# Decay weights of one superblock loaded as token pairs on two queues, with a new order of steps, in a kernel of RWKV-6 attention and a SwiGLU layer

## The chip, the cores and the metric

The kernel runs on one core of a Trainium2 chip. The metric is the device time of one execution in microseconds (us), lower is better. The kernel before took 209.78 us as the median of three runs (208.58 to 213.54). The profile is that of one execution; its span, from the first to the last instruction, is about 1.7 us shorter than the time that goes with it (208.2 for 209.92). No second core can explain anything here, so a run counts as slow only if it is more than 1.5% above the fastest of its own kernel; ratios below are of fast runs, while the medians quoted are of all runs.

## The reference, cut to what matters

```python
B, H, S, D = 4, 8, 768, 48                       # r, k, v, w: (B, H, S, D) float32
for t in range(S):                               # attention: a state of D x D per batch and head
    cur = einsum('bhd,bhe->bhde', u * kt, vt)
    y[:, :, t] = einsum('bhd,bhde->bhe', rt, state + cur)
    state = wt[:, :, :, None] * state + einsum('bhd,bhe->bhde', kt, vt)
x = y as (B*S, H*D) = (3072, 384)
xn = x / rms(x) * rms_g                          # feed-forward, 384 -> 1536 -> 384
out = (silu(xn @ w_gate) * (xn @ w_val)) @ w_out
```

## The kernel before

The sequence is cut into 6 superblocks n of 128 tokens; each has the 4 batches j. For a block (n, j), 128 tokens lie on the 128 partitions. The decays w are needed as sums of logarithms over the tokens before and after each token. ACT takes the logarithm (`ln`), PE multiplies by a triangular mask (`cs_mm`), ACT takes the exponential (`exp_r`, `exp_k`), and DVE multiplies r and k with it. When the four blocks of a superblock are done, its 512 tokens go through the feed-forward: 12 times gate group, value group, Silu, product, then 4 output groups.

The program is a list of steps, `operation.n.j`, in a fixed order; each engine runs its own instructions in that order. The parts that the change touches:

```python
def load(which, n, j):                     # r, k, v: 128 x 8 runs of 48 floats (192 bytes)
    inp[which, n, j] = pin.tile([128, H, D], FP32, name=which + "t", bufs=NIN)
    dmas["load_" + which, n, j] = nc.sync.dma_start(out=inp[which, n, j], in_=... "h t d -> t h d")

def load_w(n, j):
    paired = (n, j - j % 2) in W_PAIR
    ...                                    # one tile [128, 2*384] for two batches
    if paired:                             # partition = token pair; 64 partitions for each batch
        o = t.rearrange("p (h x) -> p h x", h=H)[PD * (j % 2):PD * (j % 2) + PD]
        src = src.rearrange("h (g i) d -> g h (i d)", i=2)
    else:
        o = t.rearrange("p (b h d) -> p b h d", b=2, h=H)[:, j % 2]
        src = src.rearrange("h t d -> t h d")
    eng = nc.scalar if paired and j % 2 else nc.sync
    ... eng.dma_start(out=o, in_=src)

ones_row = const.tile([1, 128], FP32)
i3 = small.tile([KC, KC], FP32)
if W_PAIR:                                 # masks for sums over token pairs
    mp = const.tile([128, 2, 130], BF16)
    mp_b = junk[:, 0:2 * 130]...           # a tile that exists anyway
    ...                                    # two memsets, two selects, a copy, all on POOL

def cs_pair(n, j):                         # four half-height products in place of two, for two batches
    for t, o, late in ((b, 0, 1), (a, NP, 0)):
        for i in range(2):
            for c in range(2):
                rows = slice(PD * c, PD * c + PD)
                nc.tensor.matmul(t[c][:, o:o + DM]..., lhsT=mp[rows, i, late:late + L], rhs=lw[rows, n % 2, j + i, :, 0:D], ...)
```

The paired code stood in the kernel before, but `W_PAIR = ()` kept it off. In the built program the pools lie one after the other: the constants from byte 16640 of a partition, then the persistent tiles from 20736, the input tiles (`pin`) from 79104, the work tiles (`pt`) from 128256.

## Time and profile before

| | before |
|---|---|
| time, median of 3 | 209.78 us |
| PE busy, all of it | 189.6 us of the 208.2 us span |
| first gate group starts | 29.04 us |
| PE idle from there to 160 us | 130.96 - 125.85 = 5.11 us |
| hardware queue of SyncE | 125328 packets |

The prediction reads these numbers as two stages and shows the lines. In what follows, a hole is a stretch in which PE is idle after the start of the first gate group.

### The profile page before, as it was taken

What the parts mean: (1) busy time and instruction counts of PE and PEld (TensorE: products, weight loads), DVE (VectorE), ACT (ScalarE), POOL (GpSimd) and SP (SyncE); (2) the same over time, 40 slices, a digit from 0 to 9 for tenths busy, and PEclk for the clock granted to TensorE, in tenths of its full rate; (3) what the DMA queues carried; (4) which work ended last, traced back from release to release, by engine and by line L of the source; (5) the groups of instructions that cost most, each with busy time, mean ns of one, the idle gap of its engine ahead of it and who ended that gap; (6) DMA issues with size and microseconds to landing.
All of it is one profiled execution on the core that took longest, in us unless ns stands there. A gap on an engine that the chain in (4) does not pass through costs nothing.

```text
span 208.2 us, 4362 instructions
## 1 busy us (share of the span) xinstructions
PE 189.6 (91%) x1512; PEld 110.6 (53%) x1512; DVE 156.1 (75%) x314; ACT 141.0 (68%) x290; POOL 108.9 (52%) x167
## 2 busy tenths in 40 slices
PE   5666869899999999889999999999999999999994
PEld 2444524456565555555555655555555655555563
DVE  6497855799899898869989969978997956254311
ACT  3786994678997646699637998569887973344110
POOL 3398504479789498856699692566614520000000
PEclk9995579999999999999999999999999999999999
DMA  6999999999999999899999968995467130200122
GB/s 133 212 201 204 179 201 202 186 190 225 189 209 224 135 225 190 179 260 208 177 211 205 225 150 186 168 229 107 113 176 143 38 113 3 77 0 0 39 101 91
DMA packets 127391, 32.81 MB, mean 158 GB/s; under 512 B 122244, under 2 KB 126216, under 8 KB 127368
## 3 DMA queue, kind: packets, MB, share of 16 engines
q1 hardware_dynamic: 125328, 28.98, 69.4%
q0 software_dynamic: 2032, 3.54, 9.3%
q8 instruction: 12, 0.20, 0.4%
q14 instruction: 11, 0.09, 0.1%
q10 hardware_dynamic: 8, 0.00, 0.0%
HBM read 25.96 MB, written 4.72 MB: 147 GB/s over the span
## 4 chain that ended last, share of the span: by engine, by line
PE 47%; SPq 20%; ACT 10%; DMA 7%; DVE 6%; POOL 5%; issue 3%; POOLq 0%; ACTq 0%; DVEq 0%
SPq L210 16%; PE ps_q L625 14%; PE ps_a L565 14%; PE ps_b L565 13%; SPq L227 4%; DMA rt<-in_r_dram 3%; DVE ht L583 3%; DMA kt<-in_k_dram 2%; ACT xn L528 2%; DMA wt<-in_w_dram 2%; ACT L195 2%; ACT sg L197 1%; POOL rstd L524 1%; ACT junk L515 1%; ACT ps_a L197 1%
## 5 line engine op out<-in xcount | busy, mean ns | idle before, releaser
L583 DVE TENSOR_TENSOR ht<-ps_b,sg 128x512 bf16<-128x512 f32 x72 | 49.0, 687 | 21.9 <-PE ps_b L565 17.4
L197 ACT ACTIVATE sg<-ps_a 128x512 bf16<-128x512 f32 x72 | 42.6, 596 | 32.2 <-PE ps_a L565 32.1
L565 PE MATMUL ps_a<-xnt,wg_sb 128*128 128x512 bf16 x216 | 59.4, 385 | 1.0 <-DMA wg_sb<-in_moe_w_gate_dram 0.8
L565 PE MATMUL ps_b<-xnt,wv_sb 128*128 128x512 bf16 x216 | 59.2, 383 | 0.5 <-DVE ht L583 0.5
L625 PE MATMUL ps_q<-wo_sb,ht 128*128 128x384 bf16 (+1 forms) x300 | 49.9, 319 | 0.3 <-ACT ob L634 0.3
L422 POOL TENSOR_TENSOR ruk<-rt,kt 128x384 f32<-128x384 f32 x24 | 24.6, 1024 | 23.7 <-DMA rt<-in_r_dram 17.2
L625 PEld LDWEIGHTS <-ht 128*128 128x128 bf16 x300 | 28.1, 98 | 16.7 <-issue 0.2
L565 PEld LDWEIGHTS <-wg_sb 128*128 128x128 bf16 x216 | 23.4, 115 | 21.3 <-issue 1.5
L565 PEld LDWEIGHTS <-wv_sb 128*128 128x128 bf16 x216 | 23.5, 114 | 20.7 <-issue 1.4
L432 POOL TENSOR_TENSOR ydiag<-vt,diag 128x384 f32<-128x384 f32 x24 | 19.9, 830 | 10.9 <-DMA vt<-in_v_dram 6.1
L423 POOL TENSOR_TENSOR ruk<-ruk,u_bc 128x384 f32<-128x384 f32 x24 | 24.2, 1006 | 1.9
L634 ACT COPY ob<-ps_q 128x384 f32<-128x384 f32 (+1 forms) x20 | 9.2, 473 | 14.3 <-PE ps_q L625 13.7
L464 DVE TENSOR_TENSOR qts<-ps_q,mask_lt 128x512 bf16<-128x512 f32 x24 | 16.4, 682 | 1.7 <-PE ps_q L459 1.3
L197 ACT ACTIVATE lw<-wt 128x384 bf16<-128x384 f32 x24 | 12.3, 518 | 7.2 <-DMA wt<-in_w_dram 7.1
L528 ACT ACTIVATE xn<-xb,rstd 128x384 bf16<-128x384 f32 x24 | 14.4, 608 | 3.4 <-POOL rstd L524 3.3
L475 POOL TENSOR_SCALAR_AFFINE_SELECT qts<-qts 128x512 bf16<-128x512 bf16 x20 | 13.1, 655 | 6.1 <-ACT qts L468 5.9
L510 DVE TENSOR_TENSOR xb<-ps_q,ydiag 128x384 f32<-128x384 f32 x24 | 13.1, 551 | 2.4 <-PE ps_q L505 2.3
L195 ACT ACT_TABLE_LOAD x10 | 12.8, 1283 | 1.8 <-PEq L661 1.6
L515 ACT ACTIVATE junk<-xb 128x384 bf16<-128x384 f32 x24 | 12.4, 515 | 2.1 <-DVE xb L510 1.8
L416 DVE TENSOR_TENSOR rk<-kt,ps_b 128x384 bf16<-128x384 f32 x20 | 10.9, 548 | 3.6 <-ACT ps_a L197 1.8
L411 DVE TENSOR_TENSOR rk<-rt,ps_a 128x384 bf16<-128x384 f32 x20 | 10.9, 548 | 2.7 <-DMA rt<-in_r_dram 1.2
L427 DVE TENSOR_REDUCE diag<-ruk 128x8 f32<-128x384 f32 x24 | 12.9, 542 | 0.0
(71 smaller groups left out, 262.0 us busy)
## 6 DMA issues: line engine op xcount, KB each, us to landing
wt<-in_w_dram SPq DMA_DIRECT2D x24, 192.0 KB, 3.9
vt<-in_v_dram SPq DMA_DIRECT2D x24, 192.0 KB, 3.9
kt<-in_k_dram SPq DMA_DIRECT2D x24, 192.0 KB, 3.9
rt<-in_r_dram SPq DMA_DIRECT2D x24, 192.0 KB, 3.8
out_dram<-ob SPq DMA_DIRECT2D x23, 192.0 KB, 2.7
wo_sb<-in_moe_w_out_dram POOLq DMA_DIRECT2D x3, 384.0 KB, 6.3
wv_sb<-in_moe_w_val_dram POOLq DMA_DIRECT2D x1, 768.0 KB, 10.5
wg_sb<-in_moe_w_gate_dram POOLq DMA_DIRECT2D x1, 768.0 KB, 14.0
```

The source lines that it names most:

```text
L195: nc.scalar.preload_act_table_set(table_name)
L197: return nc.scalar.activation(**kw).ins
L210: dmas["load_" + which, n, j] = nc.sync.dma_start(out=inp[which, n, j], in_=t[j, :, n * L:(n + 1) * L, :].rearrange("h t d -> t h d")).ins
L422: nc.gpsimd.tensor_tensor(out=ruk[n, j], in0=inp["r", n, j], in1=inp["k", n, j], op=ALU.mult)
L423: nc.gpsimd.tensor_tensor(out=ruk[n, j], in0=ruk[n, j], in1=u_bc, op=ALU.mult)
L432: nc.gpsimd.tensor_tensor(out=ydiag[n, j], in0=inp["v", n, j], in1=diag[n, j].to_broadcast([128, H, D]), op=ALU.mult)
L464: nc.vector.tensor_tensor(out=qts[n, j][:, 0], in0=bank["q", n, j][0], in1=bc_mid(mask_lt, NP), op=ALU.mult)
L515: nc.scalar.activation(out=junk, in_=xb[n, j], func=AF.Square, accum_out=rstd[n, j][:, 0:1])
L528: nc.scalar.activation(out=xn, in_=xb[n, j], func=AF.Copy, scale=rstd[n, j][:, 1:2])
L565: nc.tensor.matmul(ps, lhsT=units(ws, c, f), rhs=xnt[n][:, c, :], start=(c == 0), stop=(c == KC - 1))
L583: nc.vector.tensor_tensor(out=ht[n][:, f, :], in0=bank.pop(("v", n, f)), in1=bank.pop(("sg", n, f)), op=ALU.mult)
L625: nc.tensor.matmul(ps[:, cols], lhsT=ht[n][:, f, b * L:(b + 1) * L], rhs=wo_sb[:, f, cols], start=(f == 0), stop=(f == FC - 1))
```

## The change

The four w loads of superblock 1 are to use 384-byte runs (two tokens that lie side by side in memory) instead of 192-byte runs, so half as many packets. The two batches of a pair go to different halves of the partitions, one issued by SyncE, one by ACT. The price is a mask for the sums over pairs, and sums in two half-height products. The whole order of steps was made anew with it.

```diff
-    W_PAIR = ()
+    W_PAIR = ((1, 0), (1, 2))
...                                        the order: a few of its lines near the first gate group
-load_r.1.0 x_add.0.1 load_gv.0.0 q_mask_e.0.2 cast_v.0.3 load_r.1.1 xn_mul.0.0 bonus_sum.0.3 load_gv.0.1 q_mm.0.3
-ln.1.2 y_mm.0.2 bonus_v.0.3 x_sq.0.1 q_mask_e.0.3 st_mm.0.1 exp_k.1.0 w_tot.0.3 x_add.0.2 load_gv.1.1 cs_mm.1.1
+cs_mm.1.0 q_mask_e.0.2 load_v.1.0 bonus_v.0.2 cast_v.0.2 x_add.0.1 ln.1.2 bonus_sum.0.3 load_r.1.1 load_gv.0.1
+st_mm.0.1 x_sq.0.1 q_mm.0.3 st_new.0.1 exp_k.1.0 load_k.1.1 xn_pe.0.0 bonus_v.0.3 exp_r.1.0 q_mask_e.0.3 y_mm.0.2
...                                        (the other lines of the order are cut)
-        for c in (j, j + 1) if n in Q_PAIR else (j,):
+        for c in (j, j + 1) if (n, j) in Q_PAIR else (j,):
```

`Q_PAIR` is empty, so the last edit does nothing. `load_gv.g.h` loads part g of the gate weights (h = 0) or value weights (h = 1).

## The prediction

> **What bounds the kernel now.** I read the page's busy tenths first (40 slices of 5.2 us), then the busy time by windows, the timeline of the first 60 us engine by engine, and the DMA view by windows.
>
> ```profile
> PE   5666869899999999889999999999999999999994
> PEclk9995579999999999999999999999999999999999
> DMA  6999999999999999899999968995467130200122
> ```
>
> TensorE (PE) is full from slice 8 on, and the DMA engines are full from 5 us to about 125 us. So there are two regimes: a head of about 30 us in which PE is fed by what the DMAs bring and runs partly at half clock, and a body in which PE itself is the bound. The windows view puts sizes to that (columns: busy us and count of PE, its weight loads, DVE, ACT, POOL; then granted clock, DMA share, GB/s):
>
> ```profile
> 16.00:20.00 4.00, 2.51 (x30) 1.71 (x28) 3.08 (x7) 2.44 (x6) 3.35 (x5) 0.50 1.02 201
> 20.00:24.00 4.00, 3.36 (x41) 2.37 (x42) 2.98 (x8) 3.92 (x13) 3.77 (x5) 0.50 1.02 169
> 24.00:28.00 4.00, 2.29 (x20) 1.21 (x19) 3.06 (x9) 3.90 (x13) 0.00 (x0) 0.85 1.23 202
> ...
> 84.00:88.00 4.00, 3.45 (x38) 2.33 (x39) 3.56 (x9) 2.82 (x7) 3.18 (x6) 1.00 0.73 145
> 88.00:92.00 4.00, 2.99 (x35) 2.00 (x33) 2.22 (x6) 3.07 (x8) 3.21 (x6) 1.00 1.13 279
> ```
>
> ACT, not PE, is full from 20 to 28 us. From 40 us to 160 us PE's idle time, summed over the 10 us windows, is 4.3 us, of which 1.6 us lies in 84 to 92. Nothing after 160 can be won except the output tail. A gate or value group of three matmuls takes 0.65 us, an output group of twelve 1.95 us: 144 x 0.65 + 24 x 1.95 = 140 us are fixed work. The end is therefore the start of the first gate group, plus fixed PE work, plus the few holes. Those moments in the timeline:
>
> ```profile
> 18.12 0.52 ACT L197 ACTIVATE lw<-wt 128x384 bf16<-128x384 f32 x1 [1.52 <-DMA wt<-in_w_dram]
> ...
> 21.93 7.68 SPq L210 DMA_DIRECT2D vt<-in_v_dram  x1
> ...
> 29.04 1.44 PE L565 MATMUL ps_a<-xnt,wg_sb 128*128 128x512 bf16 x3
> ...
> 31.16 0.60 ACT L197 ACTIVATE sg<-ps_a 128x512 bf16<-128x512 f32 x1
> ...
> 37.09 0.84 PE L565 MATMUL ps_a<-xnt,wg_sb 128*128 128x512 bf16 x3 [0.79 <-DMA wg_sb<-in_moe_w_gate_dram]
> ```
>
> ACT waited 1.52 us for w of (1,1), then was never free until the first Silu at 31.16. PE later lost 0.8 us to the second part of the gate weights. SyncE's issue at 21.93 was stuck for 7.68 us[...].
>
> [...]between 10 and 20 us
>
> ```profile
> q1 hardware_dynamic: 10562, 2.00, 101.2%
> ```
>
> is 1.012 x 160 us / 10562 = 15.3 ns for a 192-byte packet, and in 195 to 200 us, with almost only 1536-byte output rows, 0.21 x 80 us / 288 = 58 ns: eight times the bytes for 3.8 times the time. [...]the q matmuls (48 rows each, halves at partitions 0 and 64, two banks) start in pairs, at 80.64, 80.70, 80.75 and 80.81 us, so two of 128 columns cost about 57 ns. The new decay sums have that form (64 rows, two banks).
>
> **The change part by part.**
> Transfers: the four w loads of superblock 1 go from 1024 packets of 192 bytes to 512 of 384. A load now costs 1024/16 x 15.3 = 0.98 us of all engines. With the line through 15.3 and 58 ns a 384-byte packet is about 21.5 ns (estimate), 512/16 x 21.5 = 0.69 us; if only the count mattered, 0.49. Saved: 4 x 0.29 to 0.49 = 1.2 to 2.0 us, all before 22 us, in front of the weights.
>
> ACT: four Ln of 518 ns become two of 768 columns. The 1024-column copies took 1.01 us and 384-column Exp 0.47, so 0.84 ns a column, 0.84 us each: 0.4 us saved. ACT gains two issues; such issues took 0.45 to 1.2 us on SyncE in the first 15 us: +1 to +1.8 us. In the new order the Ln pair comes behind the first normalization, so the 1.52 us wait should be filled. One more Exp (0.47) goes ahead of the last normalization. I scheduled ACT by hand with these durations: the last normalized tile is ready at about 28.2 us instead of 27.4, but no fourth decay sum stands between it and the gate. First gate at 29.2 against 29.04, Silu at 31.2 against 31.16: no gain at the start (+0.2 us).
>
> PE: two 384-column sums per block become four half-height ones, two at a time: 8 full-height slots before and 8 after; the one-column sums go from 16 to 32, also in pairs. Zero on balance. Even if serial, 8 x 0.16 us[...] falls where PE had 5.7 us of 16 idle (12 to 28 us).
>
> POOL: the pair masks are two memsets, two selects and a copy, near 0.3 us each, placed where POOL waited 4.80 us. Hidden.
>
> Order: the value weights go first, then gate, gate, value. POOL issues the first gate part only behind a bonus product that needs v of (0,3), at 22.3 us by my count instead of 19.64; but the weight queue then still has value data to move, so this part should land as the second did, at 28.4, just in time. The second gate part, which held PE at 37.09, should land about where third in line did, 32.7, and the last value part is wanted a group later: -0.8 us. PE also does a transpose, q and state sum of (1,0) between the first groups, work moved forward.
> At 84 to 92 us ACT waited 1.08 and 1.02 us for w of superblock 3. The new order has w (3,1) five loads earlier and (3,2), (3,3) two earlier. I credit half of the 1.56 us hole: -0.7.
>
> Sum: +0.2 - 0.8 - 0.7 = -1.3 us on 209.78, about 208.5; I put it at 208.4, since the shorter transfers can only help the body.
>
> **The rivals.** (a) ACT's issue gets stuck, as SyncE's did for 7.68 us at 21.93. Then ACT, full from 20 us on, delays everything: +1 to +3 us, 210 to 212. Against it: both issues come near 13 and 16 us, before the weights, into an empty queue of their own. (b) The gate weights come late through POOL's wait for v of (0,3), which now has about 1.4 more loads ahead of it: the first gate slips to 30 or 31, +1 to +2 us. For it: the first part is issued 2.7 us later. Against: the weight queue is never empty. (c) The whole saving of 1.2 to 2.0 us reaches the start, and both holes close: 3 to 4 us, 206 to 207. Against: ACT, not the DMA, is full before the gate. (d) The transfers are hidden anyway and the reordering of the body costs as much as it gains: 209 to 210. For: the DMA is full for 125 us, yet PE hardly waits.
>
> **Range and chances.** The three runs of before span 208.58 to 213.54, so noise alone is a few us. 205.8 to 211.2 holds (c) almost whole, the centre, (d) and the mild half of (a) and (b). Faster by 2% means under 205.6, more than every hole I can name: 0.11. Slower means over 214, which needs (a) and (b) together: 0.06. The rest, 0.83, is within 2%.
>
> **What would show it.** Right: 2048 fewer packets on the hardware queues; a 384-byte packet near 21 ns; Ln with 768 columns near 0.84 us; first gate within 1 us of 29; no wait for gate weights near 37; 84 to 92 us fuller. Wrong: ACT's issues over 1.2 us each, a first gate that waits for its weights, half-height sums that follow one another, a gate start before 28, or new PE holes after 40 us over the old 4.3 us.

## The result, and the profile after

The kernel after took 216.85 us as the median of four runs (216.60 to 217.21), against 209.98 (208.58 to 213.54) for the kernel before in the same rounds. A ratio in this document is the mean time of one kernel's fast runs over that of the other's of the same rounds, so not quite the ratio of the medians quoted. Here it is 1.0352, with a 95% interval of 1.0297 to 1.0406 (the slow run of 213.54 is left out). The change is slower; the prediction said 208.4 us.

The page's busy tenths of the kernel after (40 slices of 5.4 us, rows as in the prediction), and its queue lines (packets, megabytes, packet time as a share of 16 engines):

```profile
PE   5583848997999999989999699899999999999994
PEclk9999965899999999999999999999999999999999
DMA  7999999999989999999999998999467111101022
...
q1 hardware_dynamic: 122224, 28.58, 77.8%
...
q10 hardware_dynamic: 1064, 0.40, 1.2%
```

and the queue of the kernel before:

```profile
q1 hardware_dynamic: 125328, 28.98, 69.4%
```

The packets went down, as intended: 122224 + 1064 against 125328 + 8 (the 8 of the ACT queue before) is 2048 fewer. Yet the time of the packets went up, from 69.4% of 208.2 us to 77.8% of 215.5 us. That is the first sign that something happened to every packet, not only to the w loads.

The busy windows of the kernel after that answer to those in the prediction:

```profile
16.00:20.00 4.00, 0.70 (x9) 0.35 (x8) 1.56 (x5) 3.42 (x8) 0.86 (x2) 1.00 1.40 189
20.00:24.00 4.00, 3.63 (x52) 2.73 (x52) 3.73 (x9) 2.32 (x4) 3.92 (x5) 1.00 1.29 174
24.00:28.00 4.00, 2.94 (x51) 1.90 (x48) 3.95 (x9) 3.41 (x11) 2.49 (x4) 1.00 0.99 150
84.00:88.00 4.00, 3.95 (x31) 2.07 (x32) 3.92 (x9) 2.36 (x6) 3.05 (x6) 1.00 1.34 203
88.00:92.00 4.00, 4.00 (x51) 2.72 (x50) 3.92 (x8) 3.95 (x7) 3.54 (x5) 1.00 1.08 164
```

PE did 0.70 us of work between 16 and 20 us, where the kernel before did 2.51. ACT, full from 20 to 28 us before, now had 2.3 us idle there. The 84 to 92 us stretch became full, as predicted. The DMA share is at or above 1 for nearly all of it, as before, and yet the throughput from 16 to 28 us is 189, 174 and 150 GB/s against 201, 169 and 202. The timeline names the waits:

```profile
18.90 0.55 DVE L416 TENSOR_TENSOR rk<-kt,ps_b 128x384 bf16<-128x384 f32 x1 [2.13 <-DMA kt<-in_k_dram]
20.37 1.03 PE L439 MATMUL ps_q<-ident,rk 128*128 128x128 bf16 x8 [1.52 <-DVE rk L411]
...
32.96 0.62 PE L565 MATMUL ps_a<-xnt,wg_sb 128*128 128x512 bf16 x1 [0.99 <-ACT ek L197]
...
34.47 0.60 ACT L197 ACTIVATE sg<-ps_a 128x512 bf16<-128x512 f32 x1 [0.23 <-PE ps_a L565]
```

Product k of superblock 0 waited 2.13 us for its input, and the transposes behind it came at 20.37 us. The first gate group starts at 32.96 us, 3.92 us later than before, and it comes singly, with other PE work between its three products.

Where the 7.3 us between the two spans (208.2 and 215.5) went can be counted with the sum of the prediction: start of the first gate group plus holes. Two stretches, from that start to 40 us and from 40 to 160 us, have this sum (us, then the busy time of each engine), before:

```profile
sum 130.96, PE 125.85 PEld 73.03 DVE 112.83 ACT 99.21 POOL 88.46; mean PE 62.93 PEld 36.52 DVE 56.42 ACT 49.61 POOL 44.23
```

and after:

```profile
sum 127.04, PE 119.82 PEld 69.88 DVE 106.45 ACT 92.43 POOL 83.62; mean PE 59.91 PEld 34.94 DVE 53.23 ACT 46.22 POOL 41.81
```

The holes grew from 5.11 to 7.22 us, by 2.1; with the 3.9 at the start that is 6.0 of the 7.3 us. So both stages lost, and what made them lose may have acted all along the run.

To find the first moment at which the two traces differ, I went back to the earliest transfers. Up to 10 us the two kernels issue the same loads in the same order, all of superblock 0, all of 192-byte runs; the first half of a pair is issued at 10.74 us by SyncE, the second at 12.71 us by ACT:

```profile
10.74 1.02 SPq L227 DMA_DIRECT2D wt<-in_w_dram  x1
...
12.71 0.68 ACTq L227 DMA_DIRECT2D wt<-in_w_dram  x1
```

The DMA view from 5 to 10 us, before:

```profile
q1 hardware_dynamic: 5708, 1.08, 109.6%
...
rt<-in_r_dram SPq DMA_DIRECT2D x2, 192.0 KB, 4.0
```

and after (last column of the load line: median us from issue to landing):

```profile
q1 hardware_dynamic: 5016, 0.95, 143.8%
...
rt<-in_r_dram SPq DMA_DIRECT2D x2, 192.0 KB, 4.8
```

The time per packet is share x 16 engines x 5 us over the count: 1.096 x 80 / 5708 = 15.4 ns before, 1.438 x 80 / 5016 = 22.9 ns after. The packet times sum to 109.6% and 143.8% of the time of the 16 engines, so on average more than one packet of an engine was under way, and this is how long a packet lasted and not what it cost an engine: the same loads moved at 216 GB/s before and at 190 after, 12% less. Neither paired loads, nor ACT's issues, nor the new order have begun to act there. What is different already is where the destination tiles lie. The mask `mp` has 2 x 130 x 2 = 520 bytes in each partition and takes 544 (it starts at 20736, the next tile at 21280), in the pool in front of everything that is allocated later. No trace shows an address, but those in the two programs, when they are built, confirm it: `wt` moved from 79104 to 79648, `vt` from 91392 to 91936, `kt` from 103680 to 104224, `rt` from 115968 to 116512. All four were multiples of 64 and are now 32 past one.

### The profile page after: what moved, and what is told of

Read it like the earlier page. It is cut to its first block, busy times and chain, and to the rows that moved or that the text cites. A ratio compares the mean times of both kernels' runs of the same rounds, so it can differ in the third digit from the quotient of the medians.

```text
span 215.5 us, 4412 instructions
## 1 busy us (share of the span) xinstructions
PE 191.3 (89%) x1519; PEld 111.9 (52%) x1536; DVE 157.8 (73%) x314; ACT 141.2 (66%) x288; POOL 109.9 (51%) x172
## 3 DMA queue, kind: packets, MB, share of 16 engines
q1 hardware_dynamic: 122224, 28.58, 77.8%
q10 hardware_dynamic: 1064, 0.40, 1.2%
## 4 chain that ended last, share of the span: by engine, by line
PE 53%; DMA 12%; ACT 12%; SPq 9%; DVE 6%; issue 4%; POOL 3%; ACTq 0%; DVEq 0%; POOLq 0%
PE ps_a L565 18%; PE ps_b L565 16%; PE ps_q L625 13%; SPq L210 5%; DMA vt<-in_v_dram 5%; DMA rt<-in_r_dram 3%; SPq L227 3%; ACT L195 2%; DMA rkT<-rk 2%; PE ps_q L457 2%; ACT xn L528 2%; DVE rk L411 2%; DMA out_dram<-ob 1%; ACT junk L515 1%; ACT lw L197 1%
## 5 line engine op out<-in xcount | busy, mean ns | idle before, releaser
L565 PE MATMUL ps_b<-xnt,wv_sb 128*128 128x512 bf16 x206 | 58.1, 384 | 1.9 <-DVE ht L583 1.6
L625 PEld LDWEIGHTS <-ht 128*128 128x128 bf16 x300 | 28.1, 98 | 17.3 <-issue 0.9
L422 POOL TENSOR_TENSOR ruk<-rt,kt 128x384 f32<-128x384 f32 x24 | 24.1, 1004 | 19.5 <-DMA kt<-in_k_dram 10.9
L475 POOL TENSOR_SCALAR_AFFINE_SELECT qts<-qts 128x512 bf16<-128x512 bf16 x20 | 12.7, 634 | 23.2 <-ACT qts L468 22.9
L197 ACT ACTIVATE lw<-wt 128x384 bf16<-128x384 f32 (+1 forms) x22 | 11.7, 545 | 4.9 <-DMA wt<-in_w_dram 4.8
L468 ACT CAST qts<-ps_q 128x512 bf16<-128x512 f32 x20 | 11.6, 582 | 4.9 <-PE ps_q L459 4.9
```

What stands on the lines that cost most here:

```text
L197: return nc.scalar.activation(**kw).ins
L422: nc.gpsimd.tensor_tensor(out=ruk[n, j], in0=inp["r", n, j], in1=inp["k", n, j], op=ALU.mult)
L565: nc.tensor.matmul(ps, lhsT=units(ws, c, f), rhs=xnt[n][:, c, :], start=(c == 0), stop=(c == KC - 1))
L625: nc.tensor.matmul(ps[:, cols], lhsT=ht[n][:, f, b * L:(b + 1) * L], rhs=wo_sb[:, f, cols], start=(f == 0), stop=(f == FC - 1))
```

## The experiments

The theory was: 192-byte packets into destinations at 32 modulo 64 are slower, and that is most of the loss. The rivals were that the loss comes from the pairs themselves (mask sums, ACT's issues, two queues), or from the new order (above all the late weight loads). Twelve kernels ran in three groups of four, each group on one chip. The kernel before took 211.72, 212.18 and 212.04 us as the median on these three chips, more than its 209.98 on the first one; the kernel after hardly differs between chips (216.85 and 217.53). Ratios below are against the kernel before of the same group. All results were correct.

| run | kernel | median us | ratio (95%) | first gate us | 192-byte packet, 5 to 10 us |
|---|---|---|---|---|---|
| e1 | after, mask padded to 1024 | 213.34 | 1.0082 (1.0018 to 1.0146) | 31.68 | 15.5 ns |
| e2 | before, shifted by 32 | 215.89 | 1.0185 (1.0128 to 1.0242) | 31.80 | 21.4 ns |
| e3 | after, mask padded to 576 | 213.14 | 1.0033 (0.9961 to 1.0104) | 32.13 | 15.3 ns |
| e4 | new order, no pairs | 212.40 | 1.0002 (0.9933 to 1.0070) | 30.75 | 15.2 ns |
| e5 | after again | 217.53 | 1.0261 (1.0194 to 1.0329) | 33.32 | 20.2 ns |
| e6 | e1, weights in the old order | 213.39 | 1.0067 (1.0003 to 1.0132) | 30.25 | 15.2 ns |
| e7 | e1, one queue | 212.62 | 1.0054 (0.9983 to 1.0126) | 31.55 | 15.2 ns |
| e8 | old order, pairs, padded mask | 215.59 | 1.0158 (1.0070 to 1.0246) | 35.32 | 15.4 ns |
| e9 | before, only load tiles shifted | 215.17 | 1.0132 (1.0091 to 1.0172) | 31.71 | 21.9 ns |
| e10 | before, all but the load tiles shifted | 212.18 | 0.9968 (0.9905 to 1.0031) | 29.31 | 15.3 ns |
| e11 | new order, weights earlier | 215.50 | 1.0125 (1.0070 to 1.0181) | 31.68 | 15.3 ns |
| e12 | before, gate part first | 212.24 | 1.0000 (0.9956 to 1.0045) | 29.48 | 15.3 ns |

Several expectations missed their ranges. The absolute times expected of e1, e3 and e4 (207 to 211 us) were missed, on a chip on which the kernel before was 2 us slower too. The ratios of e5, e8 and e11 lie outside every range that was named, and those of e9 and e10 lie just below theirs.

**e1, the mask padded.** The same kernel with 480 more bytes behind the mask, so that all later tiles move by 1024.

```diff
         mp = const.tile([128, 2, 130], BF16)
+        const.tile([128, 240], BF16, name="pad2")
```

> The changed kernel with 480 unused bytes after its new pair mask, so that every later tile moves by 1024 bytes instead of 544 and load destinations start at 0 instead of 32 modulo 64. Theory A (placement: the 520-byte mask moves all load destinations off a 64-byte boundary, and every 192-byte packet gets slower): packets between 5 and 10 us go back from 22.9 to about 15.4 ns, first gate back near 29 us, time 207 to 210 us. Theory B (the new order itself starves the gate weights): packets may change, time stays 214 or more. Theory C (the second hardware queue slows the packets): nothing changes, 217 us.

The packet time fell back to 1.115 x 80 / 5772 = 15.5 ns:

```profile
q1 hardware_dynamic: 5772, 1.09, 111.5%
```

The time is 213.34 us, ratio 1.0082. An unused pad takes back most of the loss. The first gate group didn't come back near 29 us, as theory A had it, but only to 31.68.

**e2, the kernel before shifted by 32 bytes.** Neither pairs nor the new order; 32 bytes that nobody uses in the constants.

```diff
     nc.gpsimd.memset(ones_row, 1.0)
+    const.tile([128, 16], BF16, name="pad2")
     i3 = small.tile([KC, KC], FP32)
```

> The kernel before, with nothing changed but 32 unused bytes in front of the tiles that follow the constants; load destinations start at 32 modulo 64. Theory A: packets between 5 and 10 us go from 15.4 to about 22.9 ns, time 214 to 219 us. Theories B and C: 210 us, as before.

```profile
q1 hardware_dynamic: 5056, 0.96, 135.4%
```

Packets of 1.354 x 80 / 5056 = 21.4 ns, and 1.0185 times the time (the interval lies wholly above 1, though not wholly above 2%). The pad alone makes the kernel before lose 1.8%.

**e3, the mask padded to another multiple.** 32 bytes behind the mask, so that later tiles move by 576, a multiple of 64 but not of 128 or 256.

```diff
         mp = const.tile([128, 2, 130], BF16)
+        const.tile([128, 16], BF16, name="pad2")
```

> The changed kernel with only 32 unused bytes after the mask: tiles move by 576 bytes, so destinations are at 0 modulo 64 but no longer at 0 modulo 256 as before. Theory A with a 64-byte boundary: the same as the run with 480 bytes, 207 to 210 us, packets 15.4 ns. Theory A with a wider boundary (128 or 256): between, or still 217 us. Theories B and C: 214 to 217.

Packets of 15.3 ns and a ratio of 1.0033 (one of its four runs was slow and is left out). Here it was enough that the load tiles begin at a multiple of 64 (`wt` at 79680, not a multiple of 128 or 256): the packets are as short as the 15.5 ns of e1, where they begin at multiples of 256.

**e4, the new order without pairs.** `W_PAIR = ()`, and the steps that the pairs had swallowed are put back behind their partners.

```diff
-    W_PAIR = ((1, 0), (1, 2))
+    W_PAIR = ()
... in the order
-ln.1.0 ... cs_mm.1.0 ... ln.1.2 ... cs_mm.1.2
+ln.1.0 ln.1.1 ... cs_mm.1.0 cs_mm.1.1 ... ln.1.2 ln.1.3 ... cs_mm.1.2 cs_mm.1.3
```

> The new order with the pairs switched off: no mask, no shift, single w loads of 192-byte runs, all on SyncE; each paired Ln and decay sum stands as two in the same place. Theory A: 208 to 211 us, packets 15.4 ns. Theory B: 214 or more, with the first gate at 32 us or later. Theory C: 208 to 211.

The order alone is a tie (1.0002, one slow run left out), although the first gate group is at 30.75 us and waits for its weights:

```profile
30.75 0.62 PE L565 MATMUL ps_a<-xnt,wg_sb 128*128 128x512 bf16 x1 [0.82 <-DMA wg_sb<-in_moe_w_gate_dram]
```

**e5, the kernel after again**, unchanged, beside e6 to e8.

> The changed kernel itself, once more, on the same chip as the next three, as their yardstick. If placement is most of the loss: 1.03 to 1.035 of before, that is 2 to 2.7% above the run with the padded mask (1.008). If the first measurement was a peculiarity of its chip: within 1% of before.

217.53 us, ratio 1.0261, a little less than expected, with the granted clock at 1.00 between 30 and 40 us (0.56 in the first profile of this kernel). So that stretch of low clock isn't the cause.

**e6, the old order of the weights** in the padded kernel: both parts that the first groups need are issued at once, ahead of the bonus product of (0,3).

```diff
-... load_r.1.1 load_gv.0.1 / ... cast_v.0.3 load_gv.0.0 / ... load_gv.1.0 / ... load_gv.1.1
+... load_r.1.1 load_gv.0.0 load_gv.0.1 / ... load_gv.1.1 load_gv.1.0
```

> The changed kernel with the padded mask, and the four loads of gate and value weights put back in the order of before: both first parts ahead of the bonus product of (0,3), then value, then gate. Theory D (what remains of the loss with the padded mask is that POOL holds the first gate part until v of (0,3) has landed): first gate starts 1 to 2 us earlier than in the run with 480 bytes of padding, time 0.5 to 1.5 us below it, about 1.000 to 1.003 of before. Rival E (ACT, not the weights, sets the first gate): unchanged, 1.006 to 1.010.

The first gate group came 1.4 us earlier than in e1, at 30.25 us, and no change of the time can be seen (1.0067 and, in the other group, 1.0082; the intervals are about 0.6% wide to each side, 1.4 us, so a small gain isn't excluded). The second Silu still starts at 35.95 us, against 36.83 in e1: what follows the first group holds the start, not the weights alone.

**e7, one queue** for the pairs of the padded kernel.

```diff
-        eng = nc.scalar if paired and j % 2 else nc.sync
+        eng = nc.sync
```

> The changed kernel with the padded mask, but all four paired loads issued on SyncE in the order of the list, none on ACT. Theory F (the second queue takes its share at once and holds up r and k of (0,3), which ACT and PE wait for near 18 us): r of (0,3) lands about 0.7 us earlier, time 0.5 to 1 us below the run with 480 bytes of padding. Rival[...]: unchanged within 0.5 us.

1.0054 against 1.0067 for e6 (which differs in the weight order too) and 1.0082 for e1 (on another chip): no difference can be seen. The two logarithms of the pairs waited 1.59 and 0.98 us here, against 0.55 in all in e1, and that cost nothing that shows.

**e8, the pairs in the old order**, with the padded mask; the paired sums stand where the old order leaves room for them.

```diff
-    W_PAIR = ()
+    W_PAIR = ((1, 0), (1, 2))
         mp = const.tile([128, 2, 130], BF16)
+        const.tile([128, 240], BF16, name="pad2")
... in the order: ln.1.1, ln.1.3, cs_mm.1.1, cs_mm.1.3 dropped; cs_mm.1.0 behind w_tot.0.3, cs_mm.1.2 ahead of exp_k.1.2
```

> The kernel before in its own order, with the pairs on, the mask padded, and only what the pairs force moved: each paired decay sum stands where the second of the two stood, and one copy of decay totals is moved ahead of it. If the shorter transfers are worth what I estimated (1.2 to 2.0 us of DMA ahead of the weights) and reach the start: 0.990 to 0.996 of before. If ACT is full there and they are hidden: 0.998 to 1.004. If the pairs cost by themselves (decay sums of two blocks tied together, all four accumulators taken at once): 1.005 to 1.010.

It lost 1.6%, outside all three ranges, and the trace names a reason of its own. ACT issues one half of each pair and later waits for both halves, in order:

```profile
17.93 0.84 ACT L197 ACTIVATE lw<-wt 128x768 bf16<-128x768 f32 x1 [3.62 <-DMA wt<-in_w_dram]
...
26.20 0.84 ACT L197 ACTIVATE lw<-wt 128x768 bf16<-128x768 f32 x1 [2.01 <-DMA wt<-in_w_dram]
```

The old order has the logarithm where one batch is ready but the pair isn't. The wait of 3.62 us also held up ACT's own next load: its half of the second pair was issued at 20.82 us, SyncE's half at 17.12, and the second logarithm waited for it. The new order leaves room for the pairs: in the kernel after, the two logarithms wait 0.2 us in all.

**e9 and e10, which tiles it is.** Both are the kernel before with unused pads. In e9 only the input tiles of r, k, v and w move by 32 bytes (a second pad brings the rest back to a multiple of 64). In e10 everything behind the constants moves by 32 except these tiles.

```diff
 e9
+    pin.tile([128, 16], BF16, name="pad3", bufs=1)
+    pt.tile([128, 16], BF16, name="pad4", bufs=1)
 e10
+    const.tile([128, 16], BF16, name="pad2")
+    pin.tile([128, 16], BF16, name="pad3", bufs=1)
+    pt.tile([128, 16], BF16, name="pad4", bufs=1)
```

> The kernel before with 32 unused bytes in front of the load tiles (r, k, v, w) and 32 more behind them, so that these tiles alone start at 32 modulo 64 and every other tile stays at 0. If the slow packets come from the destinations of the loads: packets between 5 and 10 us at 22 to 23 ns instead of 15.4, time as in the run with everything shifted, 1.015 to 1.022 of before. If it is something else that moved (weights, operands of TensorE, the source of the output stores): 1.000, packets 15.4 ns.

> The complement: 32 unused bytes behind the constants, 32 in front of the load tiles, 32 behind them, so that all later tiles start at 32 modulo 64 except those of r, k, v and w, which start at 0. If the destinations of the loads matter alone: 0.998 to 1.004 of before, packets between 5 and 10 us at 15.4 ns. If other tiles matter too: 1.005 to 1.02.

The DMA view from 5 to 10 us of e9:

```profile
q1 hardware_dynamic: 5051, 0.96, 138.2%
```

and of e10:

```profile
q1 hardware_dynamic: 5466, 1.03, 104.5%
```

The load tiles alone carry the effect: 1.0132 with slow packets (21.9 ns) when they move, 0.9968 with 15.3 ns when everything else moves. The engines read these tiles too, but that isn't slower: the logarithm of 384 columns took 518 ns in e9 and 517 in e10, DVE's product with k 549 and 548, POOL's product of r and k 1011 and 1004. With the other operands of the engines, the weights and the output tiles at 32 modulo 64, e10 shows no cost (0.9968). The holes tell how it reaches the time. From the first gate group to 160 us, e9 has 128.29 - 121.06 = 7.23 us of PE idle time:

```profile
sum 128.29, PE 121.06 PEld 69.88 DVE 110.03 ACT 95.24 POOL 86.16; mean PE 60.53 PEld 34.94 DVE 55.01 ACT 47.62 POOL 43.08
```

and e10, from 29.31 us on, has 130.69 - 124.67 = 6.02:

```profile
sum 130.69, PE 124.67 PEld 71.58 DVE 110.42 ACT 97.63 POOL 86.63; mean PE 62.34 PEld 35.79 DVE 55.21 ACT 48.81 POOL 43.31
```

These two have one order, one chip and almost the same clock (1.00 and 0.99). So slow packets cost 2.4 us at the start and 1.2 us in holes after it; the two spans differ by 2.9 us. e1, whose first gate group is as late as that of e9 (31.68 us), has only 128.32 - 123.46 = 4.86:

```profile
sum 128.32, PE 123.46 PEld 72.57 DVE 110.25 ACT 96.73 POOL 83.50; mean PE 61.73 PEld 36.28 DVE 55.12 ACT 48.37 POOL 41.75
```

So a start as late as that doesn't by itself set the end: e1 ends 3.4 us before e9. It isn't that the new order had done more PE work by then (19.96 us busy before the first group, 20.44 in e9). e1 differs from e9 in the order, the pairs and the packets, and no run tells how the smaller holes divide among them.

**e11, an attempt to better the new order:** e4, with the weight parts earlier and the work of (1,0) moved behind the fourth value group.

```diff
-... load_gv.0.1 ... load_gv.0.0 ... load_gv.1.0 ... load_gv.1.1
+... load_gv.0.0 load_gv.0.1 ... load_gv.1.0 load_gv.1.1
-q_mm.1.0, q_copy_o.1.0, q_mask_e.1.0, st_mm.1.0, q_mask_o.1.0, st_new.1.0, bonus_v.1.0 between gate_mm.0.1 and val_mm.0.3
+the same seven steps behind val_mm.0.3
```

> A try at a kernel that beats both: the new order without pairs (1.0002 of before), both first weight parts ahead of the bonus product of (0,3) as before, the second gate part ahead of the second value part, and q, state sum and masks of (1,0) moved behind the fourth value group, so that no TensorE or ACT instruction waits for them between the first groups. If the head of the new order costs what the traces show (first gate 30.75 against 29.04 us, second Silu at 36.1 against 32.65): first gate near 29.5, time 0.990 to 0.997 of before. If the body takes the gain back: 0.998 to 1.003.

It failed: 1.0125 (two slow runs left out). SyncE's issue of a v load, after POOL's four issues of weights (20.68 to 26.06 us), was stuck for 10.59 us, and ACT waited for that v:

```profile
28.03 10.59 SPq L210 DMA_DIRECT2D vt<-in_v_dram  x1
...
37.51 0.51 ACT L336 CAST vb<-vt 128x384 bf16<-128x384 f32 x1 [2.48 <-DMA vt<-in_v_dram]
```

An issue is stuck in other kernels too (7.68 us in the kernel before, 8.11 in e12) without such a loss, so it may matter which load is caught. No run tests that this is the cause.

**e12, what the predicted gain at 37 us was worth:** the kernel before with the second gate part in front of the second value part.

```diff
-... x_add.0.2 load_gv.1.1 cs_mm.1.1 x_rstd.0.1 q_mask_o.0.3 exp_r.1.0 load_gv.1.0
+... x_add.0.2 load_gv.1.0 cs_mm.1.1 x_rstd.0.1 q_mask_o.0.3 exp_r.1.0 load_gv.1.1
```

> The kernel before with one change: the second part of the gate weights is loaded ahead of the second part of the value weights. It tests the step of my prediction that valued the 0.8 us wait of PE for gate weights near 37 us. If that wait is on the path: 0.995 to 0.997 of before. If PE waits for something else in its place: 0.998 to 1.002.

The busy time by 10 us of e12 (PE first):

```profile
30.00:40.00 10.00, 10.00 (x44) 4.48 (x42) 5.71 (x10) 6.18 (x10) 2.97 (x3) 1.00 1.11 208
40.00:50.00 10.00, 7.44 (x61) 4.09 (x60) 6.99 (x12) 6.13 (x11) 7.67 (x11) 1.00 0.96 181
```

and of e10, which keeps the old order, runs as fast as the kernel before and was profiled on the same chip:

```profile
30.00:40.00 10.00, 7.67 (x35) 3.59 (x34) 4.25 (x7) 5.19 (x8) 2.03 (x3) 0.90 1.06 196
40.00:50.00 10.00, 9.78 (x69) 4.99 (x67) 6.54 (x12) 6.38 (x11) 7.31 (x9) 0.93 0.98 183
```

In e10 PE waited 2.33 us for the second gate part (0.8 in the profile of the kernel before, on the first chip). In e12 that hole is closed (10.00 instead of 7.67), and one as big opened ten microseconds later (7.44 instead of 9.78), most of it where PE waited for a product of r that had waited for its own load:

```profile
49.54 0.56 DVE L411 TENSOR_TENSOR rk<-rt,er 128x384 bf16<-128x384 f32 x1 [1.96 <-DMA rt<-in_r_dram]
```

The time is the same, 1.0000. Its interval still allows the 0.8 us that the prediction credited, but not the 2.33.

## Why the prediction was wrong

**The step that failed.** "POOL: the pair masks are two memsets, two selects and a copy ... Hidden." The mask was counted as work only, not as memory. Its work was indeed hidden: five instructions of 0.30 to 0.41 us between 2.6 and 4.6 us. Its 544 bytes moved every later tile by 32 modulo 64, and with that the second number that the prediction took over unchanged fell too: "1024/16 x 15.3 = 0.98 us" for a load. A 192-byte packet took 20.2 to 22.9 ns after (5 to 10 us, e5 and the first profile; 18.7 and 19.5 over the whole run, against 16.0 before). Every load of r, k, v and w before consists of such packets, 96 x 1024 = 98304 in all, while the pairs had only 2048 to save. The size by itself: in one group, e5 over e7 is 1.0261 / 1.0054 = 1.021 and e5 over e6 is 1.019, though e6 and e7 differ from e5 in one thing more; over e1, in another group, it is 1.018. So some 2% of the 2.6% there is placement; on the kernel before alone it is 1.3% (e9) to 1.8% (e2). How much of the 3.5% on the first chip is placement, no run tells. Nor does a run tell why packets into tiles at 32 modulo 64 last longer, and between multiples of 64 no other offset was tried. None of the four rivals had the placement, and the range of 205.8 to 211.2 left no room for it. The noise of a few us that the range rests on came from one slow run; the fast ones span 208.58 to 210.18.

**What remains.** With the mask padded the kernel is at 1.0033 to 1.0082 in four kernels (e1, e3, e6, e7), whose intervals overlap with each other and in two of them hold 1. The order alone is at 1.0002. So pairs in the new order bring no gain that shows, or lose a few tenths of a per cent; these runs can't say which. The predicted gain of 1.3 us (0.6%) isn't there even without the slow packets. On the first chip the kernel before was 2 us faster than on the others and the kernel after was not, which is why 1.0352 stands there; why that chip is kinder to the kernel before is open.

**The transfers: mechanism right, size off.** The packet count fell by 2048 as predicted. In the packet records of the traces, over the stretch in which the 384-byte packets move, these lasted 26.5 ns in e7 (one queue) and 28.1 to 34.9 in the other padded kernels, and the 192-byte packets beside them 16.8 to 20.9. The ratio is 1.50 to 1.67 in all five (e7: 26.5 / 16.8 = 1.58), not 21.5 / 15.3 = 1.41: the straight line through 192 and 1536 bytes was too kind. A paired load in e7 then takes 512/16 x 26.5 = 0.85 us against 1024/16 x 16.8 = 1.08, a fifth less for half the packets (a sixth to a quarter less in the five kernels); over the five kernels the four loads save 0.9 to 1.3 us of packet time, not 1.2 to 2.0. Without the pad a 384-byte packet took 39.9 ns, and 512/16 x 39.9 = 1.28 us is more than a load took before.

**ACT: sizes right, schedule wrong.** The logarithm of 768 columns took 834 ns, predicted 0.84, and waited 0.2 us in all (columns: count | busy us, mean ns | idle before, of which on the wait named):

```profile
L197 ACT ACTIVATE lw<-wt 128x768 bf16<-128x768 f32 x2 | 1.7, 834 | 0.2 <-DMA wt<-in_w_dram 0.2
```

Its two issues took 0.68 and 0.61 us; rival (a), a stuck issue, did not happen. They were not lost time for ACT, as the prediction counted them: the first ran from 12.71 to 13.39 us, and ACT's next instruction started at 13.08. But the schedule made by hand had the last normalized tile ready at 28.2 us; it was ready at 31.4, and at 29.8 in e1 with good packets, where ACT had stood 1.43 us for the transposes of PE.

**PE: right.** The half-height sums ran side by side. The last four of them (64 rows, 384 columns each) and the one-column sums behind them in the timeline of the kernel after (start, duration):

```profile
27.33 0.69 PE L360 MATMUL ps_a<-lw,mp 64*128 64x384 bf16 x4
27.71 0.48 PE L366 MATMUL ps_a<-ones_col,lw 64*128 64x1 bf16 x16
```

The next group starts 0.38 us after the four did; one after the other they would take 4 x 0.16 = 0.64 (estimate from the 24 output products of 384 columns that took 3.90 us from 175.18 us on in the trace before). So what the q matmuls showed in the trace before, two of 128 columns in 57 ns, holds for this form too.

**The first gate group: wrong.** Predicted 29.2 us, measured 32.96. Slow packets made about 2.4 us of such a delay by themselves (e9 at 31.71, e10 at 29.31 on one chip), and the new order with the pairs had it at 31.68 with good packets. The two don't add up: together they would be more than the 3.92 us measured. Rival (b), gate weights late through POOL, was true as a mechanism: POOL issued the gate part at 26.67 us in the kernel after, not at 22.3, and e1's first gate group waited 1.33 us for it. In the kernel after itself that group waited for ACT (0.99 us) and not for its weights. And its price was put too high: e6 took that delay back and won nothing that shows.

**Order, -0.8 us: not borne out.** The wait at 37 us went, and in e12 the hole moves to the next late input, with no gain that shows. **84 to 92 us, -0.7 us: the forecast came true, but its cause isn't shown.** The stretch is full after (3.95 and 4.00 of 4). It is also full in e10, which keeps the old order:

```profile
84.00:88.00 4.00, 4.00 (x51) 2.43 (x49) 3.07 (x7) 3.26 (x5) 3.92 (x6) 1.00 1.02 202
88.00:92.00 4.00, 4.00 (x35) 2.55 (x34) 3.92 (x10) 3.20 (x10) 2.04 (x6) 1.00 0.82 200
```

In e12, also in the old order, it is 7.97 of 8. So the hole of 1.56 us belonged to the one profile that the prediction was made from, and the credit rested on that. In the kernel after, holes opened elsewhere, so the whole is 7.22 us against 5.11. Closing the hole of 2.33 us in e12 gained nothing that shows (1.0000), as the next inputs came late too; that the full DMA engines (share 1.11 and 0.96 in those 20 us of e12) are the reason is argued, not tested.

## What to carry to other kernels

A new constant tile is also an offset for every tile that is allocated after it (544 bytes here): compare the addresses of the transfer destinations before and after an edit, and try a pad that puts them back where they were; here multiples of 64 bytes were enough (15.3 ns a packet in e3, 22.9 in the kernel after). When a change makes a kernel slower, look for the earliest moment at which the traces differ; here it lay before the first paired load. And before crediting a closed wait, look in a second profile whether the wait is there again, and ask what is late behind it, since the next wait may take its place.
